# Three fixed buffers for x, written and waited for tile by tile

## The chip, the cores and the metric

The kernel runs on one NeuronCore of a Trainium2 chip. The metric is the device time of one execution in microseconds (us); lower is better. The engines are TensorE (PE, its weight loads PEld), VectorE (DVE), ScalarE (ACT), GpSimd (POOL) and SyncE (SP). Each works through its own list of instructions in order; semaphores order the lists against one another. SP and POOL also issue DMA transfers.

## The reference

Attention within chunks of 64 tokens, then a mixture of experts with two levels of routing, all in float32:

```python
scores = (q_c @ k_c^T) / sqrt(64)            # 8 batches, 8 heads, 576 tokens in 9 chunks of 64
attn   = exp(scores - max) ; attn /= (sum(attn) + 1e-9)
x      = (attn @ v_c) as 4608 rows of 512    # token by token, heads side by side
g      = argmax(x @ w_group)                 # 4 groups
e      = argmax(x @ w_expert[g])             # 4 experts in each
out[t] = p_g * p_e * (relu(x[t] @ w1[g, e]) @ w2[g, e])    # w1 512 x 1024, w2 1024 x 512
```

p_g and p_e are the softmax weights of the chosen group and expert.

## The kernel before

Two stages follow each other. The first, up to about 220 us of the span, is attention and routing; the second runs the experts over the sorted tokens.

**The attention stage** cuts the 4608 tokens into 36 tiles of 128 (two chunks each), and the tiles into nine groups of four (NG = 4). The order of its instructions is written out by hand in the strings START, MID and TAIL: a letter names a step and a number the tile, and `run` emits them one by one, so all five lists are fixed. The steps of a tile that matter here:

- a: PE transposes raw q and k (line 346), ACT and DVE copy them out of PSUM (line 395).
- b, s, e, c: scores on PE (lines 406 and 411), maximum and difference on DVE (lines 419 and 422), exponential on ACT (line 428), transposes back (346, 444).
- p: PE multiplies with v into the PSUM tile `o` (line 457, for the last tiles line 464). `o` has one buffer: the next tile's p waits until this tile's n has read it.
- n, `stage_norm`: DVE adds and inverts the sums (lines 472 and 474) and writes the 512 numbers of each token into `x` (line 482). This step is called the norm here.
- x, 1, l, 2, 3: x is transposed, multiplied with the router weights (lines 504 and 516), and DVE works out each token's row in the sorted order (`pos`, line 617) and its weight (line 580, one write for a group's four tiles).
- o, `scatter`: POOL issues an indirect DMA (line 632) that writes a tile's 128 rows of 514 numbers (512 of x, the token's number, its weight) to `xs` in DRAM. Ahead of it stands a one-element copy, the poke (line 631), which waits for the latest norm and so holds the scatter back to its place in the program. The scatter of a tile comes some 8 tiles after its norm.

**Buffers of x.** A buffer holds the four tiles of a group, [128, 4, 514]. One of the three is `xl`, which stays until the end; the two others come from the pool `xpool` with two buffers. A buffer comes round every twelve tiles. At the first tile of a group (`i == 0`) the program takes the group's buffer, and POOL writes the token numbers of all four tiles with one copy (line 479). A tile taken from a pool waits until everything that used the buffer is done, and that includes all four scatters of the group three before. The fourth of these is issued shortly ahead of the new group's first norm.

**The end of the stage.** POOL also loads the first expert's weights (lines 205 and 209), gathers its tokens (line 682) and works out part of its low halves (lines 232 and 715), in between pokes and scatters. The second stage starts when all of the first one's work, the scatters too, is done; it is one loop over units of up to 256 tokens in which PE runs nearly without a gap (lines 965 and 979).

Of the kernel before, what the change touches and what calls it, by code (L numbers as in the profile page):

```python
# [9 lines left out]
F32 = mybir.dt.float32  # L10
F32R = mybir.dt.float32r
BF16 = mybir.dt.bfloat16
I32 = mybir.dt.int32
# [6 lines left out]
P = 128  # L20
# [5 lines left out]
D = H * HD  # L26
# [4 lines left out]
NG = 4  # L31
RPE = N // P
GL = NT // NG - 1
# [4 lines left out]
XW = D + 2  # L38
# [27 lines left out]
C_ID, C_TRI, C_SEL, C_BASE, C_IOTA4, C_TID, C_T17, C_I64, C_J128, C_FORCE, C_BE, C_PBASE, C_E, C_PM, C_I16, C_PJ, C_PQ, C_PMIN, C_PNEED, C_PAR, C_N = (  # L66
    0, 128, 256, 276, 292, 296, 332, 349, 413, 449, 450, 451, 452, 453, 455, 471, 473, 475, 476, 477, 479)
# [44 lines left out]
def moe_kernel(tc, q, k, v, w_group, w_expert, w1, w2, cst, out):  # L112
    nc = tc.nc
    w1 = w1.rearrange("g e d f -> (g e) d f")
    w2 = w2.rearrange("g e f d -> (g e) f d")
    with ExitStack() as ctx:
# [5 lines left out]
        cs = wpool.tile([P, C_N], F32, name="cs")  # L122
# [9 lines left out]
        xl = wpool.tile([P, NG, XW], F32, name="xl")  # L132
# [101 lines left out]
        with ExitStack() as c1:  # L234
            cpool = c1.enter_context(tc.tile_pool(name="cp", bufs=1))
            apool = c1.enter_context(tc.tile_pool(name="at", bufs=2))
            xtpool = c1.enter_context(tc.tile_pool(name="xt", bufs=1))
            xpool = c1.enter_context(tc.tile_pool(name="xp", bufs=2))
            ppool = c1.enter_context(tc.tile_pool(name="pp", bufs=3))
            rpool = c1.enter_context(tc.tile_pool(name="rt", bufs=2))  # L240
            ps_t = c1.enter_context(tc.tile_pool(name="pst", bufs=2, space=PSUM))
# [6 lines left out]
            nc.vector.memset(off[:, E:E1], 2.0 * P)  # L248
            nc.vector.memset(cum[:, 0, :], 0.0)
            poke = cpool.tile([1, 1], F32, name="poke")  # L250
            wg = cpool.tile([P, 4, 32], F32, name="wg")
            nc.vector.memset(wg, 0.0)
            own = cpool.tile([P, VG], F32, name="vg")
# [13 lines left out]
            st, TL = {}, NT - 1  # L267
# [200 lines left out]
            def stage_norm(t):  # L468
                s = st[t]
                o = s["o"]  # L470
                rc = rpool.tile([P, 2, 4], F32, name="rc")
                nc.vector.tensor_scalar(out=rc, in0=o[..., HD], scalar1=1e-9, scalar2=None, op0=ALU.add)
                more()
                nc.vector.reciprocal(rc, rc)
                more()
                g, i = divmod(t, NG)
                if i == 0:
                    st["x", g] = xl if g % 3 == GL % 3 else xpool.tile([P, NG, XW], F32, name="x")
                    nc.gpsimd.tensor_copy(st["x", g][:, :, D].bitcast(I32), cs[:, C_TID + t:C_TID + t + NG])
                x = st["x", g][:, i, 0:D]  # L480
                to = x.rearrange("p (b j d) -> p b j d", b=2, d=HD) if t < BLK else x.rearrange("p (h x d) -> p x h d", x=2, d=HD)
                nc.vector.tensor_tensor(out=to, in0=o[..., 0:HD],
                                        in1=rc.unsqueeze(3).broadcast_to([P, 2, 4, HD]), op=ALU.mult)
                more()
                s["x"] = st["lastx"] = x
                done.append(t)
# [236 lines left out]
            def more(n=1):  # L723

                for _ in range(n):
                    while routing and next(routing[0], True):
                        routing.pop(0)
# [25 lines left out]
            def run(seq):  # L753
                g = dict(P=prep_hi, j=prep_lo, J=lambda i: prep_lo(i, nc.vector), X=first_x, U=first_xl, E=exponent, L=first_l1, H=first_hi, D=first_lo, W=prep2_hi, w=prep2_lo, y=lambda i: prep2_lo(i, nc.vector), F=first_loads, R=reload, V=load_v, C=load_cst,
                         Q=load_qk, G=load_wg, Z=prefill, a=stage_a)
                f = dict(o=stage_o, b=stage_b, s=stage_sub, c=stage_ct, e=stage_exp, p=stage_pv, n=stage_norm, x=stage_xt)
                for z in seq.split():
                    if z[0] == "m":
                        more(int(z[1:]))
                    elif z[0] in g:  # L760
                        g[z[0]](int(z[1:]))
                    elif z[0] == "1":
                        stage_e1(int(z[1:]))
                    elif z[0] == "l":
                        stage_lts(int(z[1:]))
                    elif z[0] == "2":
                        stage_e2(int(z[1:]))
                    elif z[0] == "3":
                        stage_e3(int(z[1:]))
                    elif 0 <= int(z[1:]) < NT:  # L770
                        f[z[0]](int(z[1:]))
# [823 lines left out]
```

## Time and profile before

| | |
|---|---|
| median of 3 runs | 666.16 us (665.98 to 666.64) |
| the profiled execution | 667.7 us, of which the span of the trace is 666.1 us |
| busy in the span | PE 607.3 us (91%), PEld 512.2 (77%), DVE 444.3 (67%), ACT 346.7 (52%), POOL 194.7 (29%) |
| chain that ended last, by engine | PE 72%, DVE 10%, DMA 8%, ACT 4% |
| of it the transfers xs<-x,pos, the scatters | 3% |
| busy time of POOL's copies at line 479 | 1.1 us for the 6 into x, 0.6 us for the 3 into xl |

Read it stage by stage: the shares are means over a stage in which DVE, ACT, PE and the transfers take turns, and one that is all PE. The chain of waits goes back from the last instruction to whatever released each step, so a transfer in it is one for which an engine of the chain stood still. Busy time of an engine off that chain says little. In a row of the timeline the brackets give the engine's idle time ahead of the instruction and what ended it.

### The profile page before, as it was taken

The page shows a single profiled execution, that of the slowest core. Times are in us where ns is not written, and L with a number is a line of the kernel's source. Part 1 is how long each engine was busy: PE and PEld are TensorE (multiplying, and loading weights), DVE is VectorE, ACT ScalarE, POOL GpSimd, SP SyncE. Part 2 cuts the span into 40 slices and gives each one's busy share as a digit, 9 for nine tenths or more (in the row PEclk, how much of TensorE's full clock was granted, in tenths as well). Part 3 has the DMA queues.
Part 4 walks back from the last instruction along what each step waited for, and adds up shares of the span by engine and source line. Part 5 has one row for each costly group of instructions (what it writes and reads, how often), then busy time and mean ns, then how long its engine had stood idle before and what let it go on. Part 6 is the DMA issues. An engine that isn't in the chain of part 4 may idle for free.

```text
span 666.1 us, 15819 instructions
## 1 busy us (share of the span) xinstructions
PE 607.3 (91%) x5152; PEld 512.2 (77%) x5153; DVE 444.3 (67%) x792; ACT 346.7 (52%) x524; POOL 194.7 (29%) x294
## 2 busy tenths in 40 slices
PE   5887887858887899999999999999999999999996
PEld 4766676646776778888888888888888888888884
DVE  5688687947766578851577886674663888977331
ACT  4786766646663255721357565372631656644211
POOL 9000222233527233211134523232212233413220
PEclk9999989969987899999999999999999999999999
DMA  9999966994545489751085976736261368861110
GB/s 247 231 272 263 231 189 181 241 243 130 158 141 198 143 298 319 270 196 63 24 297 180 360 239 233 245 106 248 94 229 59 137 242 311 280 231 59 36 32 32
DMA packets 104493, 128.00 MB, mean 192 GB/s; under 512 B 49342, under 2 KB 72126, under 8 KB 104448
## 3 DMA queue, kind: packets, MB, share of 16 engines
q1 hardware_dynamic: 93312, 92.71, 45.8%
q0 software_dynamic: 11136, 34.69, 14.7%
q8 instruction: 28, 0.46, 0.3%
q14 instruction: 17, 0.14, 0.1%
HBM read 106.23 MB, written 21.93 MB: 192 GB/s over the span
## 4 chain that ended last, share of the span: by engine, by line
PE 72%; DVE 10%; DMA 8%; ACT 4%; issue 3%; POOL 2%; SPq 0%; POOLq 0%; DVEq 0%; ACTq 0%
PE py L979 27%; PE ph L965 14%; PE pxt L965 5%; PE ph L948 5%; DMA xs<-x,pos 3%; PE tp L346 3%; PE lgk L965 3%; PE o L457 2%; PE sc L406 2%; DVE m L419 2%; DVE pr L422 2%; ACT qT L395 2%; PE pxt L864 2%; PE ph L910 2%; DVE ktb L395 1%
## 5 line engine op out<-in xcount | busy, mean ns | idle before, releaser
L1503 POOL DMA_INDIRECT out_dram<-xl,io x37 | 41.1, 1112 | 148.0 <-DVE xl L1213 131.6
L965 PE MATMUL ph<-xt,w1h 128*128 128x512 f32 x280 | 76.3, 394 | 0.9 <-issue 0.5
L1227 DVE TENSOR_TENSOR w2l<-w2r,w2h 128x1024 fp32r<-128x1024 f32 x60 | 69.5, 1218 | 2.7 <-ACT w2h L1168 2.0
L1150 ACT ACTIVATE hth<-ph 128x512 fp32r<-128x512 f32 x28 | 16.8, 599 | 102.6 <-PE ph L965 83.2
L1223 DVE TENSOR_TENSOR w1l<-w1r,w1h 128x2048 fp32r<-128x2048 f32 x28 | 64.0, 2292 | 8.8 <-ACT w1h L1126 7.1
L979 PE MATMUL py<-w2h,hth 128*128 128x512 f32 x264 | 67.6, 398 | 0.0
L979 PE MATMUL py<-w2l,hth 128*128 128x512 f32 x264 | 65.3, 389 | 0.0
L979 PE MATMUL py<-w2h,htl 128*128 128x512 f32 x264 | 65.2, 389 | 0.0
L979 PEld LDWEIGHTS py<-w2l,hth 128*128 128x128 f32 x264 | 49.6, 188 | 10.5
L979 PEld LDWEIGHTS py<-w2h,htl 128*128 128x128 f32 x264 | 49.6, 188 | 10.3
L1126 ACT CAST w1h<-w1r 128x2048 fp32r<-128x2048 f32 x28 | 53.5, 1913 | 5.5 <-DMA w1r<-in_moe_w_dram 3.7
L965 PEld LDWEIGHTS ph<-xt,w1h 128*128 128x128 f32 x280 | 48.9, 189 | 8.6 <-issue 0.7
L979 PEld LDWEIGHTS py<-w2h,hth 128*128 128x128 f32 x264 | 47.6, 188 | 10.1 <-ACT hth L1198 0.9
L1130 ACT CAST w2h<-w2r 128x2048 fp32r<-128x2048 f32 x28 | 52.6, 1935 | 1.2 <-DMA w2r<-in_moe_w_dram 1.2
L1213 DVE TENSOR_SCALAR xl<-py,io 128x512 f32<-128x512 f32 x33 | 24.5, 748 | 36.6 <-PE py L979 36.5
L965 PEld LDWEIGHTS ph<-xt,w1l 128*128 128x128 f32 x280 | 43.0, 188 | 6.2 <-DVE w1l L1223 0.3
L1497 POOL COPY ion<-xgr 128x2 int32<-128x2 int32 x22 | 10.2, 465 | 127.7 <-PE pxt L864 116.7
L965 PE MATMUL ph<-xt,w1l 128*128 128x256 f32 x280 | 44.7, 281 | 0.1
L395 ACT COPY qT<-tp 64x512 f32<-64x512 f32 x56 | 35.4, 632 | 16.6 <-PE tp L346 15.6
L1254 DVE TENSOR_TENSOR xl<-ph,xl 128x512 f32<-128x512 f32 x28 | 19.3, 691 | 35.0 <-ACT xl L1150 32.9
L1266 DVE SCALAR_TENSOR_TENSOR htl<-xl,hth 128x512 fp32r<-128x512 f32 (+1 forms) x56 | 37.7, 673 | 2.9
L406 PE MATMUL sc<-ktb,qT 128*64 128x128 f32 x448 | 33.3, 292 | 6.5 <-DVE pr L422 2.6
(292 smaller groups left out, 1258.9 us busy)
## 6 DMA issues: line engine op xcount, KB each, us to landing
w2r<-in_moe_w_dram SPq DMA_DIRECT2D x30, 1024.0 KB
w1r<-in_moe_w_dram SPq DMA_DIRECT2D x29, 1024.0 KB, 4.9
xgr<-xs POOLq DMA_DIRECT2D x38, 257.0 KB, 3.3
qk<-in_q_dram SPq DMA_DIRECT2D x15, 512.0 KB
qk<-in_k_dram SPq DMA_DIRECT2D x15, 512.0 KB
w1r<-in_v_dram SPq DMA_DIRECT2D x24, 128.0 KB
w2r<-in_v_dram SPq DMA_DIRECT2D x24, 128.0 KB
w1r<-in_moe_w_dram POOLq DMA_DIRECT2D x3, 1024.0 KB
```

The costliest lines, as they stand in the source:

```text
L395: y.append((nc.vector.tensor_copy if not i and (z or a and FOUR <= n < 8 * B) else nc.scalar.copy)(to, at))
L406: nc.tensor.matmul(sc[HALF[c], hp], lhsT=st["T", u, 0][:, hp, k0:k0 + CH], rhs=st["T", u, 1][:, hp, :, k0:k0 + CH], start=True, stop=True)
L948: m = pe.matmul(ph[n], a_[:, c, 0:P], w_[:, c, n * 512:(n + 1) * 512], start=(i == 0), stop=(i == 11))
L965: m = pe.matmul(o if i < 4 else o[:, 0:256], (w1l if i > 3 else w1h)[:, c, f * P:(f + 1) * P], both[:, c] if i < 4 else xth()[:, c, :], st ...
L979: m = pe.matmul(py[j], a_[:, f, half[j]], w_(b, f), start=(i == 0), stop=(i == 23))
L1126: lambda b, s, j: ac.copy(wt[b][0][:, s], w1r[j]), K1, js)
L1130: lambda b, s, j: ac.copy(wt[b][2 + j], w2r[j]), K2)
L1213: return ve.tensor_scalar(out=yb[:, j, :], in0=py[j], scalar1=io[:, j, 1:2], scalar2=None, op0=ALU.mult)
L1223: lambda b, s, j: ve.tensor_sub(wt[b][1][:, s], w1r[j], wt[b][0][:, s].bitcast(F32)), K1, js)
L1227: m = ve.tensor_sub(wt[b][4 + 2 * j + i], w2r[j][:, 2 * i:2 * i + 2], wt[b][2 + j][:, 2 * i:2 * i + 2].bitcast(F32))
L1266: m = ve.scalar_tensor_tensor(out=o, in0=z[:, :, i], scalar=0.0, in1=h[:, :, i].bitcast(F32), op0=ALU.max, op1=ALU.subtract)
L1503: gp.indirect_dma_start(out, bass.IndirectOffsetOnAxis(ap=io[:, j, 0:1].bitcast(I32), axis=0), yb[:, j, :], None, bounds_check=N - 1, oob_ ...
```

## The change

The pool `xpool` goes. Its two buffers are allocated once beside `xl`, as `x0` and `x1`, and stay for the whole stage. Group g uses the buffer g % 3, as before. POOL's copy of token numbers is made for each tile by itself (36 copies of one column in place of 9 of four), at the tile's norm. All lines after the first edit move up by one: line 482 is 481 in the changed kernel, 479 is 478, 631 is 630, 632 is 631.

```diff
--- before.py
+++ after.py
@@ -235,7 +235,6 @@
             cpool = c1.enter_context(tc.tile_pool(name="cp", bufs=1))
             apool = c1.enter_context(tc.tile_pool(name="at", bufs=2))
             xtpool = c1.enter_context(tc.tile_pool(name="xt", bufs=1))
-            xpool = c1.enter_context(tc.tile_pool(name="xp", bufs=2))
             ppool = c1.enter_context(tc.tile_pool(name="pp", bufs=3))
             rpool = c1.enter_context(tc.tile_pool(name="rt", bufs=2))
             ps_t = c1.enter_context(tc.tile_pool(name="pst", bufs=2, space=PSUM))
@@ -248,6 +247,7 @@
             nc.vector.memset(off[:, E:E1], 2.0 * P)
             nc.vector.memset(cum[:, 0, :], 0.0)
             poke = cpool.tile([1, 1], F32, name="poke")
+            xbufs = [xl if i == GL % 3 else cpool.tile([P, NG, XW], F32, name="x%d" % i) for i in range(3)]
             wg = cpool.tile([P, 4, 32], F32, name="wg")
             nc.vector.memset(wg, 0.0)
             own = cpool.tile([P, VG], F32, name="vg")
@@ -474,9 +474,8 @@
                 nc.vector.reciprocal(rc, rc)
                 more()
                 g, i = divmod(t, NG)
-                if i == 0:
-                    st["x", g] = xl if g % 3 == GL % 3 else xpool.tile([P, NG, XW], F32, name="x")
-                    nc.gpsimd.tensor_copy(st["x", g][:, :, D].bitcast(I32), cs[:, C_TID + t:C_TID + t + NG])
+                st["x", g] = xbufs[g % 3]
+                nc.gpsimd.tensor_copy(st["x", g][:, i, D:D + 1].bitcast(I32), cs[:, C_TID + t:C_TID + t + 1])
                 x = st["x", g][:, i, 0:D]
                 to = x.rearrange("p (b j d) -> p b j d", b=2, d=HD) if t < BLK else x.rearrange("p (h x d) -> p x h d", x=2, d=HD)
                 nc.vector.tensor_tensor(out=to, in0=o[..., 0:HD],
```

DVE's list around the norms of tiles 24 and 25 (`x` is the buffer, `rc` the inverted sums, DMASW0 to DMASW7 the semaphores of POOL's own transfers, which take turns), before:

```order
L474 RECIPROCAL rc<-rc 128x8 [waits DVE_49]
L482 TENSOR_TENSOR x<-o,rc 128x512 [waits DMASW6_49,DMASW5_49,DMASW7_49,DMASW4_49,DVE_49]
L395 COPY kT<-tp 64x512 [waits PE_49,Activation_49]
L395 COPY qT<-tp 64x512 [waits PE_49]
L395 COPY kT<-tp 64x512 [waits Activation_49]
L472 TENSOR_SCALAR rc<-o 128x8
L474 RECIPROCAL rc<-rc 128x8 [waits DVE_49]
L482 TENSOR_TENSOR x<-o,rc 128x512 [waits DVE_49,Pool_49]
```

The same place after:

```order
L474 RECIPROCAL rc<-rc 128x8 [waits DVE_49]
L481 TENSOR_TENSOR x_121<-o,rc 128x512 [waits DMASW4_49,DVE_49,Pool_49]
L395 COPY kT<-tp 64x512 [waits PE_49,Activation_49]
L395 COPY qT<-tp 64x512 [waits PE_49]
L395 COPY kT<-tp 64x512 [waits Activation_49]
L472 TENSOR_SCALAR rc<-o 128x8
L474 RECIPROCAL rc<-rc 128x8 [waits DVE_49]
L481 TENSOR_TENSOR x_121<-o,rc 128x512 [waits DMASW5_49,DVE_49,Pool_49]
```

DVE's order is the same. The group's first norm waited for four scatters and its second for POOL; now the first waits for one scatter and the second for the next.

POOL's list where the first expert's second weight matrix is loaded (`w2r`; `w1l` is a low half, `xl,pos` a scatter), before:

```order
L632 DMA xs<-xl,pos 75904x514 [waits DMASW7_49,DMASW6_49,DVE_49]
L631 COPY poke<-x 1x1 [waits DVE_49,Pool_49]
L632 DMA xs<-xl,pos 75904x514
L232 TENSOR_TENSOR w1l_2595<-w1r,w1h_2594 128x512 [waits DMASW3_49,Activation_49]
L209 ISA
L209 DMA w2r<-in_moe_w_dram 128x4x512 [waits DMAHW4_49,DMAHW5_49,DMAHW3_49,DMAHW6_49,DMAHW2_49,DMAHW7_49,DMAHW1_49,DMAHW0_49]
```

The same place after:

```order
L631 DMA xs<-xl,pos 75904x514 [waits DMASW7_49,DMASW6_49,DVE_49]
L478 CAST x_122<-cs 128x1 [waits DMASW2_49]
L630 COPY poke<-x_122 1x1 [waits DVE_49,Pool_49]
L631 DMA xs<-xl,pos 75904x514
L232 TENSOR_TENSOR w1l_2609<-w1r,w1h_2608 128x512 [waits DMASW3_49,Activation_49]
L209 ISA
L209 DMA w2r<-in_moe_w_dram 128x4x512 [waits DMAHW4_49,DMAHW5_49,DMAHW3_49,DMAHW6_49,DMAHW2_49,DMAHW7_49,DMAHW1_49,DMAHW0_49]
```

One copy of token numbers has come in, between a scatter and the next poke; the rest of the piece stands as it did.

## Rows read from the trace of the kernel before

**Rows 1.** Waits, whole span: who waited for whom; us, times, longest.

```profile
POOL x L479 <- DMA xs<-x,pos: 13.5, 3, 5.3
...
DVE x L482 <- DMA xs<-x,pos: 10.4, 3, 4.6
PE o L457 <- DVE x L482: 10.1, 3, 4.8
...
ACT w2h L712 <- DMA va<-in_v_dram: 4.8, 1, 4.8
```

**Rows 2.** Chain of waits, 74 to 92 us: start, us, what.

```profile
77.62 6.11 DMA xs<-x,pos
...
83.75 0.05 DVEq L482
```

**Rows 3.** Timeline: start, us, engine, line, [idle before]; first stall.

```profile
80.41 0.19 DVE L474 RECIPROCAL rc<-rc 128x8 f32<-128x8 f32 x1
...
80.80 1.07 PE L504 MATMUL lgk<-xT,wg 128*32 128x512 f32 x8
...
83.84 0.69 DVE L482 TENSOR_TENSOR x<-o,rc 128x512 f32<-128x512 f32 x1 [3.10 <-DMA xs<-x,pos]
...
84.68 2.00 PE L457 MATMUL o<-w2r,pT 128*64 128x130 f32 x16 [2.82 <-DVE x L482]
...
90.83 0.69 DVE L419 TENSOR_REDUCE m<-sc 128x8 f32<-128x512 f32 x1 [1.28 <-PE sc L406]
```

**Rows 4.** Timeline, second stall.

```profile
102.40 0.19 DVE L474 RECIPROCAL rc<-rc 128x8 f32<-128x8 f32 x1
...
102.79 1.07 PE L504 MATMUL lgk<-xT,wg 128*32 128x512 f32 x8
...
105.48 0.69 DVE L482 TENSOR_TENSOR x<-o,rc 128x512 f32<-128x512 f32 x1 [2.75 <-DMA xs<-x,pos]
...
106.32 1.11 PE L457 MATMUL o<-w1r,pT 128*64 128x130 f32 x16 [2.46 <-DVE x L482]
...
110.99 0.69 DVE L419 TENSOR_REDUCE m<-sc 128x8 f32<-128x512 f32 x1
```

**Rows 5.** Timeline, third stall.

```profile
142.10 1.12 PE L346 MATMUL tp<-cs,qk 64*128 64x64 f32 x16
...
142.41 0.20 DVE L474 RECIPROCAL rc<-rc 128x8 f32<-128x8 f32 x1
...
147.19 0.69 DVE L482 TENSOR_TENSOR x<-o,rc 128x512 f32<-128x512 f32 x1 [4.57 <-DMA xs<-x,pos]
...
148.03 2.00 PE L457 MATMUL o<-vg,pT 128*64 128x130 f32 x16 [4.81 <-DVE x L482]
...
151.01 1.85 PE L504 MATMUL lgk<-xT,wg 128*32 128x512 f32 x8
```

**Rows 6.** Windows: us, PE PEld DVE ACT POOL busy, PEclk, DMA share, GB/s.

```profile
84.00:88.60 4.60, 3.92 (x40) 3.49 (x40) 4.30 (x8) 2.60 (x5) 1.22 (x3) 0.63 0.70 246
148.00:152.80 4.80, 4.77 (x41) 2.76 (x41) 2.10 (x5) 1.25 (x2) 1.93 (x3) 0.52 0.84 232
```

**Rows 7.** DMA in 40 slices of the span, page part 2.

```profile
DMA  9999966994545489751085976736261368861110
```

**Rows 8.** Line 632: time to landing.

```profile
DMA to landing us min/median/max: 3.1/5.1/7.4
```

**Rows 9.** Timeline of POOL, 125 to 178 us.

```profile
125.26 0.19 POOL L479 CAST xl<-cs 128x4 int32<-128x4 f32 x1 [4.45 <-DMA xs<-xl,pos]
125.39 0.18 POOL L631 COPY poke<-xl 1x1 f32<-1x1 f32 x1
...
177.35 1.63 POOL L209 DMA_DIRECT2D w2r<-in_moe_w_dram  x2
```

**Rows 10.** Timeline, 199 us: DVE beside POOL.

```profile
199.14 1.61 DVE L548 TENSOR_TENSOR one<-one,mx 128x80 f32<-128x80 f32 x1
...
199.36 1.29 POOL L232 TENSOR_TENSOR w1l<-w1r,w1h 128x512 fp32r<-128x512 f32 x1
```

## The prediction

> **What bounds the kernel now.** I read the waits of the whole span first, then the chain of waits, then the timeline around each wait that named x, and last the windows and the transfers.
>
> In the waits the reader is to see that two lines of the edited step wait for scatters: the norm on DVE three times, 10.4 us in all, and POOL's copy of token numbers three times, 13.5 us; PE then waits for those norms three times, 10.1 us [rows 1]. That PE's sum is nearly DVE's says that the wait is passed on in full. The chain of waits confirms that the first of them is on the path that sets the end: it runs through 6.11 us of a scatter into the norm's semaphores [rows 2]. The timelines show the three places. The inverted sums are ready at 80.60, 102.59 and 142.61, but the norms start at 83.84, 105.48 and 147.19, after 3.10, 2.75 and 4.57 us of idle DVE; PE's product with v for the next tile needs the bank that the norm frees, and starts 0.84 us after it each time [rows 3 to 5]. These are the first tiles of groups 3, 4 and 6. The two groups that go into xl (5 and 8) do not come from the pool; there only POOL waited, and DVE did not.
>
> The second stage, after about 220 us, has no x buffer in it; what the first stage gains moves it forward as a whole.
>
> **The change, part by part.**
>
> *The wait at a group's first norm.* It now asks for one scatter, that of the tile twelve before, and no longer for the one nine before. In POOL's order a group's first scatter stands four tiles ahead of the norm that needs it where the last stood one ahead. Four tiles take 21.6 us (83.84 to 105.48) [rows 3, 4], and a scatter lands in 3.1 to 7.4 us [rows 8]. So each of the 24 waits should be met when it is reached, and what is late next is PE.
>
> First stall. PE's router product ends at 80.80 + 1.07 = 81.87, by when the bank would be free (80.74 + 0.84 = 81.58). The product with v starts there and not at 84.68: 2.8 us. Beyond that the first stall has a second cost. From PE's restart to the maximum at 90.83 it took 6.15 us, and 4.67 us for the same work after the second stall (106.32 to 110.99) [rows 3, 4]. The granted clock was 0.63 in that stretch after the first stall, and the product with v took 2.00 us, against 1.11 after the second [rows 3, 4, 6]: PE was at the lower of its levels (1.2 GHz) for part of it. Without the rest the 1.48 us go too. Sum 4.3 us; bounds 2.8 and, if DVE alone decides, 3.10 + 1.48 = 4.6.
>
> Second stall. 106.32 less (102.79 + 1.07 = 103.86) is 2.5 us; the idle time of DVE, 2.75, is the upper bound.
>
> Third stall. PE's transposes end at 142.10 + 1.12 = 143.22, the norm would end at about 142.62 + 0.69 = 143.31, and PE restarts at 148.03: 4.7 us. Behind this stall PE was at 1.2 GHz up to 152.8, with a granted clock of 0.52 [rows 6]: the product with v took 2.00 us and the router product 1.85 [rows 5], against 1.11 and 1.07 [rows 4], 1.7 us more in the two. If PE works on in place of resting, some of that may be at 2.4 GHz. No row says how much; I take half, 0.8 us, between 0 and 1.7.
>
> The Trainium skill, "TensorE: Matmul & The Clock Gate", section "Part 1: The HAM clock gate", says that PE's clock is halved after idling and given back after sustained work. By that rule the whole 1.7 us of the third stall would come back, and the sum would be 12.4 us where I have 11.5. The trace agrees in the first stall and not in the second, where PE rested for 2.46 us and came back at full speed [rows 4].
>
> *27 more copies on POOL.* Nine copies become 36. A copy lasted 0.19 us, and the poke behind it started 0.13 us after it [rows 9]. I take 0.2 us for each that is on the path; a copy of one column was not measured, and its bounds are 0 (it can't save anything) and these 0.2. Six of the added ones stand at the program's start, where POOL has nothing to do but them. Most others stand just ahead of a poke that waits for a norm anyway, and that wait hides them. I find two that nothing hides: one between two scatters ahead of the load of w2r, which was issued at 177.35 [rows 9] and for which ACT, and then PE, stood 4.8 us [rows 1]; and one in the row of scatters at the stage's end, ahead of the last load of w1r. 2 x 0.2 = 0.4 us. If the cover were gone everywhere it would be 27 x 0.2 = 5.4 us. Queued behind a copy on POOL are its poke, its scatter and, from 140 us on, the weight loads and the gather; its wait for a scatter twelve tiles back is met as the norm's is.
>
> *More semaphores at the norms.* Each of 24 norms now has a transfer to ask for, and those from tile 20 on POOL as well (the poke that read that place twelve tiles earlier, long done). The semaphores ahead of the first stalled norm took 0.05 us with their transfer already landed [rows 2]. 24 x 0.05 = 1.2 us on DVE; I take 0.4 us of it on the path, with bounds of 0 and 1.2, since DVE shares the path with PE and ACT.
>
> *The waits of POOL that vanish* (13.5 us at the pool's buffers, more at xl) are worth nothing of their own: the poke behind each waits for the norm.
>
> **Sum:** 4.3 + 2.5 + 4.7 + 0.8 - 0.4 - 0.4 = 11.5 us. The profiled execution took 667.7 us, 1.6 more than its span; 667.7 - 11.5 = 656.2. It was 1.5 us above the median of the runs, so I forecast 666.16 - 11.5 = 654.7 us.
>
> **The rivals.**
>
> 1. *Loads become the next thing late.* The transfers were busy in 9 tenths or more of the slices from 117 to 150 us, and in 6 tenths from 83 to 117 [rows 7]. Squeezed into less time, those around the third stall (q, k, v, the first w1r) might not keep pace: its 5.5 us would come back, and the time would be 654.7 + 5.5 = 660.2 us. Against it: the waits name no load of q, k or v for PE at these places, and from 150 us on the transfers are busy in only 4 to 5 tenths.
>
> 2. *Copies and DVE block each other.* In one row DVE's small operation took 1.61 us while POOL ran a 1.29 us operation that reads SBUF [rows 10], so the two can shut each other out. A copy can hold DVE no longer than it lasts: if all 27 did, 27 x 0.2 = 5.4 us less the 0.4 already counted, 659.7 us. Against it: the norms that ran beside POOL's copies took their usual 0.69 us [rows 3 to 5]. The Trainium skill has this as a rule ("SBUF — State Buffer", section "Who interferes with whom"): VectorE and GpSimd share a pair of ports under an exclusive lock. It names DVE operations with two inputs in SBUF, as this one; a norm reads one of its inputs from PSUM.
>
> 3. *A fixed time later on swallows it.* ACT already stands for w2r [rows 1]. If that load landed at its old time whatever went before, all the gain would be waited away there: 666.2 us. Against it: its issue hangs on scatters and low halves that move with the rest, and the transfers had room.
>
> 4. *The places stay tied.* If a tile's write still waited for its whole buffer, only the costs would be left: 666.16 + 0.8 = 667.0 us or, with the copies well covered, no change. Against it: in the list after, each norm asks for one transfer, the next one for each next tile.
>
> 5. *Slower: scatters that land late.* Each tile from 12 on now depends on its own scatter, on DVE and POOL both, and POOL's copy stands in front of the poke and scatter that a later tile depends on. If landing took longer than the four tiles between, every tile would wait, and the scatters behind would slip too. It decides from a landing of about 17 us (21.6 less the first stall's 4.3); at 1 us for each of 24 norms the time would be 654.7 + 24 = 678.7 us. Against it: the longest landing is 7.4 us [rows 8].
>
> **How the numbers follow.** Forecast 0.78, loads 0.09, blocking 0.04, fixed time 0.03, tied places 0.02, late scatters or the like 0.04. Best case of the forecast: 4.6 + 2.75 + 4.7 + 1.7 = 13.8 with no costs, 652.4 us; I go to 651 for small savings that follow a steadier PE. Its worst within reason: 2.8 + 2.5 + 4.7 - 0.4 - 1.2 = 8.4, 657.8 us. The range reaches over rivals 1 and 2 to 661, which leaves out 0.09 and what the estimates miss. A measurement of this kernel tells about 0.2%, 1.3 us, from no change. Faster: 0.78 + 0.09 + 0.04 = 0.91; same: the fixed time and the tied places, 0.05; slower 0.04.
>
> **What would show it.** In the profile after: no wait of the norm or of the token copies for a scatter; PE's product with v within 0.1 us of its router product at the first two places; a granted clock of 1.00 around the first; 36 copies of at most 0.2 us; the wait of ACT for w2r still there, 11 us earlier; the second stage as long as before. The forecast is wrong if that wait of ACT grows by several us, if PE waits for loads of q, k or v, or if DVE's norms grow longer than 0.69 us.

## The result and the profile after

The changed kernel took 656.17 us in the median of 4 runs (654.79 to 657.90), the kernel before 666.4 us (665.98 to 666.76) beside it: a ratio of 0.9848, interval [0.9823, 0.9873], a gain of 8.5 to 11.8 us. The forecast was 654.7 us with a range of 651 to 661. The profiled execution took 654.8 us with a span of 652.7; that of before took 667.7 and 666.1. Ratios here and below leave out a run that is over 1.5% slower than the fastest of its kernel, which is one: 668.38 us, the profiled run of the kernel before with w2r loaded earlier.

The waits of the whole span of the changed kernel (who waited for whom; us, times, longest), its rows for POOL's pokes behind the norm (now L481), for scatters, and for the first w2r:

```profile
POOL poke L630 <- DVE xl L481: 25.8, 5, 12.5
POOL poke L630 <- DVE x L481: 20.8, 10, 2.7
...
POOL xg0r L681 <- DMA xs<-x,pos: 4.9, 1, 4.9
ACT w2h L711 <- DMA w2r<-in_moe_w_dram: 4.7, 1, 4.7
```

Both waits for scatters of [rows 1], that of the norm and that of the copies, are gone, and of PE's wait of 10.1 us 0.3 are left. ACT's wait for w2r has stayed at its size. (In [rows 1] the same wait carries the name of a v transfer; the waiting instruction reads w2r, and the name of the releaser is inferred.)

Timeline of the changed kernel at the first place (start, us, engine, line, [idle before]), against [rows 3]:

```profile
80.58 0.19 DVE L474 RECIPROCAL rc<-rc 128x8 f32<-128x8 f32 x1
80.83 0.68 DVE L481 TENSOR_TENSOR x<-o,rc 128x512 f32<-128x512 f32 x1
...
80.97 1.07 PE L503 MATMUL lgk<-xT,wg 128*32 128x512 f32 x8
...
81.97 1.11 PE L457 MATMUL o<-w2r,pT 128*64 128x130 f32 x16
...
86.46 0.69 DVE L419 TENSOR_REDUCE m<-sc 128x8 f32<-128x512 f32 x1 [0.33 <-PE sc L406]
```

The norm starts 0.06 us after the inverted sums, and the product with v where the router product ends (80.97 + 1.07 = 82.04). From the product to the maximum it takes 4.49 us, not 6.15: the slow clock of [rows 6] is gone too. The second place, against [rows 4]:

```profile
98.33 0.68 DVE L481 TENSOR_TENSOR x<-o,rc 128x512 f32<-128x512 f32 x1
...
98.47 1.07 PE L503 MATMUL lgk<-xT,wg 128*32 128x512 f32 x8
...
99.47 1.11 PE L457 MATMUL o<-w1r,pT 128*64 128x130 f32 x16
...
103.97 0.69 DVE L419 TENSOR_REDUCE m<-sc 128x8 f32<-128x512 f32 x1 [0.34 <-PE sc L406]
```

Here too the product with v starts where the router product ends (98.47 + 1.07 = 99.54).

At the third place, against [rows 5]:

```profile
132.84 1.54 PE L457 MATMUL o<-vg,pT 128*64 128x130 f32 x16
...
134.92 0.69 DVE L481 TENSOR_TENSOR x<-o,rc 128x512 f32<-128x512 f32 x1
...
135.76 1.59 PE L457 MATMUL o<-vg,pT 128*64 128x130 f32 x16 [0.33 <-DVE x L481]
...
137.28 0.71 PE L346 MATMUL tp<-cs,qk 64*128 64x64 f32 x16
137.92 1.06 PE L503 MATMUL lgk<-xT,wg 128*32 128x512 f32 x8
```

PE rests 0.33 us where it rested 4.81. It is still at the lower clock for part of the product with v (1.59 us against 1.11 at full speed), but the transposes behind it take 0.71 us, not 1.12, and the router product 1.06, not 1.85. PE was at the lower clock ahead of this place already, in both kernels: the product ahead took 1.54 us here, and before:

```profile
140.16 2.00 PE L457 MATMUL o<-vg,pT 128*64 128x130 f32 x16
```

The granted clock of two stretches of the changed kernel (PE, PEld, DVE, ACT, POOL busy, PEclk, DMA share, GB/s), against [rows 6]:

```profile
84.00:88.60 4.60, 4.47 (x83) 3.89 (x82) 4.03 (x13) 4.10 (x8) 1.36 (x3) 1.00 0.89 301
135.00:139.80 4.80, 4.47 (x66) 3.20 (x62) 3.02 (x6) 3.54 (x6) 3.89 (x8) 0.81 1.02 248
```

The copies (duration ns min/median/max, first and last start us), and below them from line 631 the time to landing, against [rows 8]:

```profile
L478 POOL CAST x<-cs x24: 183/200/232, 16.6 to 168.0; 128x1 int32<-128x1 f32 x24
L478 POOL CAST xl<-cs x12: 183/203/218, 17.5 to 194.2; 128x1 int32<-128x1 f32 x12
...
DMA to landing us min/median/max: 4.0/5.5/9.8
```

The last scatters of the first stage, after and before:

```profile
L1506 POOL DMA_INDIRECT xs<-xl,pos x4: 959/962/963, 207.7 to 211.5; - x4
L1507 POOL DMA_INDIRECT xs<-xl,pos x4: 960/962/963, 221.3 to 225.1; - x4
```

They start at 207.7 us and not at 221.3, and the second stage then takes 445.0 us to the end of the span (before 444.8): what was gained in front arrived at the end whole.

Between the two profiled executions the places can be added up with one mark behind each. The maximum behind the first stall came 90.83 - 86.46 = 4.4 us earlier; that behind the second (110.99, now 103.97) 7.0 earlier, 2.6 more; the end of the router product behind the third (152.86, now 138.98) 13.9 earlier, 6.9 more. The forecast terms were 4.3, 2.5 and 5.5. This pair differs by 13.4 us of span, more than the medians do; the second traces below bear on that.

### The profile page after: what moved, and what is told of

Same layout as the page of the kernel before. It is cut to its first block, busy times and chain, and to the rows that moved or that the text cites. A ratio compares the mean times of both kernels' runs of the same rounds, so it can differ in the third digit from the quotient of the medians.

```text
span 652.7 us, 15838 instructions
## 1 busy us (share of the span) xinstructions
PE 604.9 (93%) x5152; PEld 509.9 (78%) x5153; DVE 444.7 (68%) x792; ACT 346.4 (53%) x524; POOL 195.1 (30%) x321
## 4 chain that ended last, share of the span: by engine, by line
PE 67%; DMA 4%; DVE 3%; issue 2%; ACT 2%; POOL 1%; DVEq 0%; POOLq 0%; ACTq 0%; SPq 0%
PE py L978 28%; PE ph L964 14%; PE pxt L964 5%; PE ph L947 5%; PE lgk L964 3%; DMA w2r<-in_moe_w_dram 2%; PE pxt L863 2%; PE tp L346 1%; PE tp L215 1%; PE ph L909 1%; PE py L932 1%; DMA xs<-xl,pos 1%; PE o L464 1%; PE o L457 1%; PE sc L411 1%
## 5 line engine op out<-in xcount | busy, mean ns | idle before, releaser
L978 PEld LDWEIGHTS py<-w2h,hth 128*128 128x128 f32 x264 | 47.6, 188 | 10.1 <-ACT hth L1197 0.9
L1496 POOL COPY ion<-xgr 128x2 int32<-128x2 int32 x22 | 8.2, 375 | 127.9 <-PE pxt L863 116.4
## 6 DMA issues: line engine op xcount, KB each, us to landing
w1r<-in_moe_w_dram POOLq DMA_DIRECT2D x3, 1024.0 KB, 10.2
```

Source lines behind the costliest of these rows:

```text
L978: m = pe.matmul(py[j], a_[:, f, half[j]], w_(b, f), start=(i == 0), stop=(i == 23))
```

## The experiments

The runs of one group were taken on one chip, beside runs of the kernel before on the same chip: group 1 (before 666.19 us, 23 runs), group 2 (663.95 us, 11 runs), group 3 (665.86 us, 15 runs).

| kernel | median us (runs) | ratio to before | interval |
|---|---|---|---|
| group 1: the change again | 656.01 (6) | 0.9846 | [0.982, 0.9873] |
| copies tile by tile, pool kept | 666.29 (12) | 0.9988 | [0.9963, 1.0012] |
| only groups 3, 4 keep their place | 662.53 (12) | 0.9944 | [0.9919, 0.997] |
| only groups 6, 7 keep their place | 659.84 (6) | 0.9912 | [0.9885, 0.9939] |
| group 2: fixed buffers, one copy per group | 653.38 (6) | 0.9843 | [0.9804, 0.9881] |
| the change, w2r loaded earlier | 650.13 (6) | 0.9775 | [0.9745, 0.9806] |
| group 3: before, w2r loaded earlier | 661.37 (11) | 0.9932 | [0.9906, 0.9957] |
| fixed buffers, one copy per group, w2r earlier | 650.58 (6) | 0.9774 | [0.9739, 0.9809] |
| the change, third time | 655.71 (6) | 0.985 | [0.9815, 0.9884] |

**The change again.** No edit.

> The changed kernel once more, for more runs and a second trace; its first four runs lay between 654.8 and 657.9 us, the kernel before between 666.0 and 666.8. If the spread belongs to the change (work that now meets sooner or later from run to run), runs again spread over 2 to 3 us with a median of 655.5 to 657; if it was the first chip, they lie within 1 us of one another. The second trace should again show no wait of the norm for a scatter, and the end of the first stage 13 to 14 us earlier than before (its last scatters begin at 207 to 209 us where they began at 221).

0.9846; the third time, in group 3, 0.985:

> The changed kernel beside the other two on the same chip: 0.984 to 0.986 of the kernel before, with ACT's wait for w2r at 4 to 6 us. The version with early loads of w2r and one copy for each group should stand 4 to 5 us below it.

The effect is the same in all three sets of runs, and 10.2 us (666.19 - 656.01) in group 1. The six runs of group 1 again spread over 3.3 us, so the spread is not the first chip's. In the second trace no norm waits for a scatter, and ACT waits 5.8 us for w2r. Its last scatters begin at 209.3 us, a little later than expected; in a second trace of the kernel before (below) they begin at 217.0. The third place differs from the first trace, with PE at the lower clock to the end of the router product (1.86 us), though here it rested only 0.75 us:

```profile
135.39 2.00 PE L457 MATMUL o<-vg,pT 128*64 128x130 f32 x16 [0.75 <-DVE x L481]
```

The best version of group 3 stands 5.1 us below the change.

**Copies tile by tile, pool kept.**

```
                 if i == 0:
                     st["x", g] = xl if g % 3 == GL % 3 else xpool.tile(...)
-                    nc.gpsimd.tensor_copy(st["x", g][:, :, D]..., cs[:, C_TID + t:C_TID + t + NG])
+                nc.gpsimd.tensor_copy(st["x", g][:, i, D:D + 1]..., cs[:, C_TID + t:C_TID + t + 1])
```

> The pool stays, only the copies of token numbers are made tile by tile. Theory of the prediction: the three stalls stay as they are, and 27 copies cost 0.4 us with a bound of 0.8: 666.4 to 667.2 us. Rival, the copies shut DVE out (27 x 0.2): 671 us. Rival, the copies apart are what helped and the buffers are not: 656 us.

No change (0.9988). The waits of this kernel are those of [rows 1]:

```profile
POOL x L479 <- DMA xs<-x,pos: 12.0, 3, 4.7
...
DVE x L482 <- DMA xs<-x,pos: 9.8, 3, 4.9
PE o L457 <- DVE x L482: 9.5, 3, 5.1
```

27 more copies alone cost or save nothing beyond 0.4%. With the pool kept, a tile still waits for all four scatters of its buffer.

**The first two stalls alone, and the third alone.** The groups named keep the place of the group three before; the others come from the pool as before.

```
+                if g in (3, 4):          # the other kernel: (6, 7)
+                    st["x", g] = st["x", g - 3]
+                    nc.gpsimd.tensor_copy(st["x", g][:, i, D:D + 1]..., cs[:, C_TID + t:C_TID + t + 1])
-                if i == 0:
+                elif i == 0:
```

> Only groups 3 and 4 keep the place of the group three before (with copies tile by tile); groups 6 and 7 take a buffer of the pool and wait for all its scatters. Theory: the first two stalls go (4.3 + 2.5 us as forecast, 4.5 + 2.8 by the landmarks of the first trace), the third stays: 666.3 - 7.0 = 659.3 us (658.5 to 660). Rival, the third wait only grows by what the first two give (a fixed time behind it): 666 us. Rival, the first two were hidden by something else and the third is everything: 665 us or more.

> Only groups 6 and 7 keep the place of the group three before; groups 3 and 4 wait for all scatters of their buffer. Theory: the third stall goes alone, 5.5 us as forecast and 6.8 by the landmarks of the first trace: 666.3 - 6.5 = 659.8 us (659 to 661). If the third's gain needs the first two (the clock comes back sooner only when PE rests less before), 661.6 us: 4.7 us alone. If the terms add up, the gains of this run and of the one with the first two give together the gain of the whole change, to 1 us.

The first two gave 3.7 us (interval 2.0 to 5.4), not 6.8: 662.53 us lies above the expected 658.5 to 660 and below both rivals (665 us or more, 666). The third gave 6.4 (4.1 to 7.7), as expected. Together that is 10.1, which agrees with the change's 10.2 as far as the intervals go, some 2 us each. The kernel with the first two stalls gone still has the third, here longer than in [rows 5]:

```profile
141.33 0.69 DVE L485 TENSOR_TENSOR x<-o,rc 128x512 f32<-128x512 f32 x1 [5.60 <-DMA xs<-x,pos]
...
142.17 2.00 PE L457 MATMUL o<-vg,pT 128*64 128x130 f32 x16 [5.84 <-DVE x L485]
```

Either the third stall grows when the first two go and swallows part of their gain, or the first two cost less in most executions than in the one profiled. Two single executions (662.56 and 661.5 us, no ratio) look at that.

> The kernel before once more, for a second trace. Theory: the three stalls are as long as a scatter's landing, which depends on the traffic, so their sum differs from 10.4 us by 1 or 2 us from execution to execution, and this is where much of the spread of the kernel before (662.6 to 671.7) comes from. Rival: the sum is 10.4 within 0.3 us and the spread is elsewhere.

> The kernel in which only the first two stalls are taken away, for a second trace. In its first trace the third stall had grown from 4.57 to 5.60 us. Theory, with the same transfers pressed into less time the scatter that the third stall waits for lands later: again 5 us or more, and longer than in the second trace of the kernel before. Rival, chance: as likely shorter than longer.

The kernel before, a second execution, first and second place:

```profile
80.39 1.06 PE L504 MATMUL lgk<-xT,wg 128*32 128x512 f32 x8
...
82.48 0.69 DVE L482 TENSOR_TENSOR x<-o,rc 128x512 f32<-128x512 f32 x1 [2.15 <-DMA xs<-x,pos]
...
83.32 1.11 PE L457 MATMUL o<-w2r,pT 128*64 128x130 f32 x16 [1.87 <-DVE x L482]
...
87.98 0.69 DVE L419 TENSOR_REDUCE m<-sc 128x8 f32<-128x512 f32 x1
...
101.67 0.69 DVE L482 TENSOR_TENSOR x<-o,rc 128x512 f32<-128x512 f32 x1 [1.75 <-DMA xs<-x,pos]
...
102.51 1.11 PE L457 MATMUL o<-w1r,pT 128*64 128x130 f32 x16 [1.46 <-DVE x L482]
```

And its clock in the 4.6 us around the first of them:

```profile
82.00:86.60 4.60, 3.15 (x52) 2.84 (x54) 3.82 (x8) 2.38 (x5) 1.35 (x3) 1.00 0.86 287
```

The stalls are shorter than in [rows 3, 4] (3.10 and 2.75 us), and PE came back at full speed. From PE's restart to the maximum it took 4.66 us (83.32 to 87.98), not 6.15. By the forecast's own working the two stalls are worth 1.87 + 1.46 = 3.3 us here, which agrees with the 3.7 measured. The third stall was 5.08 us in this execution; with the first two gone it was 5.60 in one and 4.73 in another, where 5 us or more was expected, so its growth isn't shown.

The idle time of DVE ahead of the norms of groups 3, 4 and 6 in every execution that has them ("-": taken away there), and the time from PE's restart behind the first to the maximum, with the granted clock of that stretch; all times in us:

| | execution | group 3 | group 4 | group 6 | restart to maximum (clock) |
|---|---|---|---|---|---|
| before, as forecast from | 667.70 | 3.10 | 2.75 | 4.57 | 6.15 (0.75) |
| before again | 662.56 | 2.15 | 1.75 | 5.08 | 4.66 (1.00) |
| copies tile by tile | 671.70 | 2.53 | 2.39 | 4.90 | 6.79 (0.60) |
| before, w2r earlier | 668.38 | 2.92 | 2.03 | 5.27 | 7.04 (0.57) |
| groups 6, 7 fixed | 658.05 | 1.85 | 2.42 | - | 4.67 (1.00) |
| groups 3, 4 fixed, twice | 662.84, 661.50 | - | - | 5.60, 4.73 | - |

The execution that the forecast was read from had the longest first stall, the longest second and the shortest third. That is part of why its terms were large. The other part is the clock: the lower level behind the first stall came in three of the five executions, and in two of them it cost more than the 1.48 us of the forecast:

```profile
85.99 1.11 PE L457 MATMUL o<-w2r,pT 128*64 128x130 f32 x16 [2.24 <-DVE x L482]
...
92.78 0.69 DVE L419 TENSOR_REDUCE m<-sc 128x8 f32<-128x512 f32 x1 [2.23 <-PE sc L406]
```

This is the kernel with copies tile by tile (92.78 - 85.99 = 6.79 us). PE's rests at the two places and this cost together, the forecast's own working, come to 6.5 to 6.8 us in these three executions and to 3.3 and 3.7 in the two others. The three took 1.5, 5.4 and 7.0 us more than the medians of their kernels, the two others 1.4 and 1.8 less. So the 3.7 us measured fit executions without that fall of the clock, and the forecast's 6.8 those with it. This comes out if most executions are of the first kind; no trace shows how many are.

**Fixed buffers, one copy per group.** The change with the old copy.

```
-                nc.gpsimd.tensor_copy(st["x", g][:, i, D:D + 1]..., cs[:, C_TID + t:C_TID + t + 1])
+                if i == 0:
+                    nc.gpsimd.tensor_copy(st["x", g][:, :, D]..., cs[:, C_TID + t:C_TID + t + NG])
```

> The three fixed buffers of the change, but one copy of token numbers for a group's four tiles, at its first tile, as before. That copy waits for all four scatters of the group before it in the buffer, and the second norm of groups 3, 4 and 6 waits for the copy; the first norm waits for one scatter. Theory, the buffers' lifetime is the whole gain: DVE goes past the first norm, and by the second, 4 us later, the scatters have nearly landed, so 655.5 to 657.5 us, and POOL still waits some 4 us at each of these copies. Rival, the copies tile by tile are needed too: DVE stands at the second norm in place of the first, about 1 us in each of groups 3 and 4 and 2 or more in group 6, 660 us or more.

0.9843, as the change. Its waits:

```profile
POOL x L479 <- DMA xs<-x,pos: 11.9, 3, 4.8
...
PE o L457 <- DVE x L482: 1.8, 2, 1.1
...
DVE x L482 <- POOL x L479: 0.9, 1, 0.9
```

POOL still waits 11.9 us for the scatters, and this costs little: the norm's own place is long free, and it waits for the copy 0.9 us in all. The gain is in the buffers' lifetime and not in the copies, as far as the interval goes (some 2.5 us either way).

**The wait that was left: w2r loaded earlier.** F4 and F5, the two loads of w2r in the hand-written order, move up right behind F3, the gather.

```
-  ... x26 e28 F3 a65 e29 p27 ...  a71 F4 x28 b32 E0 m2 F5 X0 s32 ...
+  ... x26 e28 F3 F4 F5 a65 e29 p27 ...  a71 x28 b32 E0 m2 X0 s32 ...
```

> The changed kernel with the two loads of w2r (first expert) moved up on POOL, from behind two scatters and a low half to right behind the gather of the first expert's tokens. ACT stood 4.7 and 5.8 us for this load in the two traces of the changed kernel, and PE with it. Theory, this wait is the next fixed piece of the path: the load ends before ACT asks for it, ACT's wait goes to under 1 us, and the time falls by 4 to 5 us to 651.5 us (650.5 to 653). Rival, the transfers or the scatters behind it on POOL take its place: 655 to 657 us, with the wait found at a scatter's landing or a later load.

> The kernel before, with only the two loads of w2r issued right behind the gather of x, as in the version of the change that measured 0.9775. If ACT's wait for w2r is a cost of its own, it is worth here what it was worth behind the change: 4 to 5 us (ratio 0.993), and ACT's wait for w2r is gone from the list while the three stalls stay at 9 to 10 us together. If that wait decides only once the stalls are gone (it is what is late next, not what is late now), the gain is under 1.5 us here. If the early loads take transfer time from the scatters at the third stall, that stall grows by 1 us or more and eats part of it.

> Fixed buffers, one copy for each group, and the two loads of w2r issued right behind the gather. If copies tile by tile are worth nothing either way, this takes the same time as the version with 36 copies (ratio 0.9775 on another chip), 0.976 to 0.980. If the wait for the whole group's places is what the copies take away, it is 1 us or more slower than that.

With the loads moved the change gained 663.95 - 650.13 = 13.8 us. What the loads are worth behind fixed buffers is read from pairs that also differ in the copies, which cost nothing that was seen: 3.3 us in group 2 (653.38 - 650.13) and 5.1 in group 3 (655.71 - 650.58). On the kernel before, stalls and all, the loads alone gave 4.5 us (interval 2.9 to 6.3). The wait is a cost of its own in both. The change's chain of waits already had it (start, us, what):

```profile
162.24 1.23 POOL w1l L232
163.47 6.57 DMA w2r<-in_moe_w_dram
...
170.11 0.10 ACT w2h L711
```

With the loads moved, the issue and ACT's cast of the same kernel:

```profile
153.62 1.53 POOL L209 DMA_DIRECT2D w2r<-in_moe_w_dram  x2
...
166.12 0.62 ACT L711 CAST w2h<-w2r 128x512 fp32r<-128x512 f32 x1
```

ACT no longer waits ahead of the cast. The stalls of the kernel before stay when only the loads move (DVE's wait for scatters 10.2 us, 3 times). With one copy per group the time is the same, 0.9774 against 0.9775 though on another chip. These two, at 650 us, are the fastest found.

## Why the prediction was right, point by point

**The wait at a group's first norm goes, and nothing takes its place.** Right. No norm waits for a scatter in the profile after; PE's product with v starts within 0.1 us of the end of the router product at the first two places. That copies alone give nothing and fixed buffers alone give all shows the buffer's lifetime as the cause.

**First and second stall, 4.3 + 2.5 us.** Too large: 3.7 measured, and 6.8 is outside its interval. The step that failed was to take the terms of one execution, which stood 1.5 us above the median, off the median as they were. The mechanism held in that execution (4.4 and 2.6 by the marks). But its first two stalls were the longest of five, and the slow clock behind the first, 1.48 us, was counted as if every execution had it; two of the five did not.

**Third stall, 4.7 + 0.8 us.** 6.4 measured, with an interval (4.1 to 7.7) that holds 5.5, so no error is shown in it. Its stall was the shortest of all seen. Of the 1.7 us that the lower clock cost, (2.00 - 1.59) + (1.85 - 1.06) = 1.2 came back in this pair, between the half taken and the whole. Over the seven executions without this stall, what came back went from nothing (2.00 and 1.86 us in the second trace of the change) to the whole (1.11 and at most 1.07 in four). With the stall in place, the router product once took 1.11 us (before again). The Trainium skill ("TensorE: Matmul & The Clock Gate", section "Part 1: The HAM clock gate") has the clock halved after idling and given back after sustained work, which by the prediction's reading would have given the whole; the traces agree in four of the seven executions, in part in two, and not at all in one.

**The sum, 11.5 us,** against 10.2 in group 1 and 8.5 to 11.8 by the interval: the first two terms were 3.1 too large, the third, by the median, 0.9 too small, and of the costs of 0.8 nothing was seen in the time. That the total came out better than its terms is in part luck.

**27 copies, 0.4 us.** Not to be told from nothing (copies alone 0.9988 [0.9963, 1.0012]). They lasted 0.18 to 0.23 us, a little over the 0.2 named. **More semaphores, 0.4 us:** the semaphore events ahead of the norms took a median of 0.106 us and at most 0.301, over the 0.05 assumed:

```profile
L481 DVEq EVENT_SEMAPHORE  x24: 21/106/301, 80.7 to 190.8; - x24
```

Most of that was covered. At the first two places the norm starts 0.06 us after its sums. From tile 20 on it starts a median of 0.09 us after them where it was 0.04, some 0.6 us on DVE in all by the two traces. What of this is on the path was not measured by itself.

**The rivals.** Loads late (1): in the profile after PE waits for q and k only in the first 19 us, long ahead of the first place (in the second trace once more, 0.5 us at 40). Copies blocking DVE (2): the norms took 681 to 693 ns in all 36 tiles, and copies alone cost nothing. A fixed time (3): ACT's wait for w2r was real, and the piece most worth moving next, but in the profile after ACT had the load 14 us earlier (170.11, before 184.53); it was no fixed time. Tied places (4): the waits vanished. Late scatters (5): landing grew to 9.8 us at most, while the four tiles between two first norms took 17.5 us (80.83 to 98.33), and no norm waited for a scatter.

## What to carry to other kernels

A buffer taken anew from a pool waits for the last use of all of it; where its parts are used at different times, a buffer that stays and is waited for part by part took the wait for the scatters off the path here without a byte more of memory. A stall that ends with a transfer can differ from one execution to the next: here by a fifth (third place) to two fifths (first place) of its longest. What the clock costs behind it can differ more (0 to 2.4 us at the first place). Size it from several executions, and set a total against a median only when its terms are medians too. Where a stall is removed, look for the next late transfer in the list of waits; here moving the two loads of one weight matrix was worth another 3 to 5 us, with the stalls or without.

## What was not expected of the hardware

The first stall lasted 1.85 to 3.10 us over five executions. The granted clock from PE's restart behind it to the maximum was 0.75 where PE had rested for 2.82 us, 0.57 for 2.64, 0.60 for 2.24 and 1.00 for 1.87 and for 1.57. At the second place PE came back at full speed after 2.46 us [rows 4], so the length of the rest alone doesn't tell.

The runs also spread less without the stalls: the standard deviation was 2.4, 2.1 and 2.0 us for the kernel before in the three groups and 2.5 with copies alone, against 1.5 with either part of the stalls gone, 1.2 and 1.0 with all gone and 1.3 with w2r earlier as well. But fixed buffers with one copy per group spread by 2.6, by one of the six runs (658.89 us), and the kernel before with w2r earlier, all its stalls in place, by 1.4 without the run of 668.38 us (2.6 with it). Nor does the time follow the stalls' lengths: the three add up to 10.4 us in the execution of 667.70 us, to 9.8 in that of 671.70 and to 9.0 in that of 662.56. The longer runs of the kernel before show the lower mean granted clock (0.965 to 0.983 over 49 runs; correlation with the time -0.56, -0.82 and -0.50 in the three groups). So what carries the spread is open, and the clock is as good a candidate as the landings.
